# S4D layer and routed experts on one core: comparisons of places on 16-bit numbers, and another written order

## The chip, the cores and the metric

The kernel runs on one core of one Trainium2 chip. The metric is the time of one execution on the device in microseconds. The core has five engines that run beside each other, each with its own queue of instructions: TensorE (products; in the profile PE, its weight loads PEld), VectorE (DVE), ScalarE (ACT), GpSimd (POOL, here for gathers and scatters by index) and SyncE (SP, which issues the other transfers). Sixteen DMA engines move the data.

## The reference

Two layers with a residual each, on 2048 tokens of 512 channels. The first is a state-space convolution (S4D), computed in the reference with an FFT; the second sends each token to the best one of eight experts.

```python
def _A_ref(u, log_A_real, A_imag, C_real, C_imag, log_dt, D_skip):
    ...
    P = jnp.exp((A * dt[:, None])[:, :, None] * pos[None, None, :])
    K = 2.0 * jnp.einsum("dn,dnl->dl", C, P).real
    ...
    return y + u * D_skip[None, None, :]

def _B_ref(x, wg, w1, w2):
    gates = _softmax(xt @ wg, axis=-1)
    topk_idx = jnp.argsort(-gates, -1)[:, :K]      # K = 1
    ...
    h = _gelu(jnp.einsum("nd,edf->nef", xt, w1))
    y = jnp.einsum("nef,efd->ned", h, w2)
    out = jnp.einsum("ne,ned->nd", cw, y)

h = x + _A_ref(_layernorm(x), ...)
h2 = h + _B_ref(_layernorm(h), B_wg, B_w1, B_w2)
```

## The kernel before

**Stages.** The front (0 to about 125 us) loads the input in four pieces (l_x), takes the statistics of each token (u_stats, u_mean, u_dev, u_var, u_std, u_rstd), writes the normalised input (u_norm) and transforms it in two steps (u_s1, u_s2), while VectorE and ScalarE build the first tables of the convolution's kernel (t_e, t_f, t_vf, t_wi, t_wr and others). The main part goes over four blocks of 128 channels. For each block it finishes the tables, multiplies them out (t_kg, t_kt), transforms the result (c_s1, c_ev1, c_s2), multiplies with the transformed input that it loads from DRAM (c_load, c_z), transforms back (c_ia, c_ys), and sends the result through DRAM for a change of layout: c_yst writes it to yd_scratch, c_y1 loads it in four pieces, c_ib does the last small transform, c_add (L781) adds the residual. The finished block goes to DRAM (r_hd, into hd_scratch), and TensorE adds its share to the router's products (r_tr, r_ev, r_lg).

**The router.** When the last block is done, r_le and r_lt bring the products of tokens and experts into the right layout, and r_a finds each token's expert (oh). r_ag, r_sd and r_rs finish the mean and the reciprocal deviation of each token (the tile val), and r_vs (L1097) writes val into the last four columns of hd_scratch, four numbers in each of 2048 rows. r_p1, r_p1e and r_p2 count the tokens of each expert that stand ahead of each token. For the expert that runs first, r_c0, r_B0, r_t0 and r_i0 turn these counts into the list of its tokens: place p of the list is found by comparing the low part of each token's place (lo0) with 0 to 127 (is_lo, L1167), which gives a table B of zeros and ones for 16 tokens per partition, in two halves of 1024 comparisons, and by multiplying B with the tokens' numbers on TensorE (L1176). r_i0 (L1180) writes the index gi0. m_ga (L1285) gathers the token rows with it. Later r_c, r_M, r_B, r_tb and r_ix do the same for all experts; r_B uses the same is_lo, and o_b (L1258) a comparison of its own.

**The experts.** Each expert has up to 288 tokens in up to three chunks. m_ln (L1327) normalises the gathered rows (hn), m_tr (L1333) transposes them on TensorE, m_xh (L1340) and m_xl (L1345) split them into a high and a low part. Weights come in pieces of 512 KB (m_w1 L1365, m_w2 L1369), ScalarE takes their high part (m_h, L1373), VectorE the low part (m_l, L1377). m_g1 (L1386 to L1388) forms the first product from three products of the parts, m_ge, m_gh (L1394) and m_gl (L1398) apply gelu and split again, m_g2 forms the second product. The result is scattered to the output rows.

**What sets the order.** Each step is added as a task with an engine, an estimated cost, what it reads and what it writes (`plan.add`, called `at`). The table ORD gives every task's place, written out by hand as one list of 2045 places; ON says for some tasks whether VectorE (V) or ScalarE (A) does them; FILL puts idle products (L950) ahead of some tasks of TensorE. The program is issued in the order of ORD, so each engine's queue is in that order, and an instruction waits in its queue until what it reads is there and the buffer that it writes is free. The lists r= and w= in the calls decide only which buffer of a ring a task takes; the waits follow from the tiles themselves.

Buffers that matter here: c_y1's loads of blocks 0 to 2 share one buffer (y1), block 3's results three (ys3), the expert's r1 and r2 three each.

Of the kernel before, what the change touches and what calls it, by code (L numbers as in the profile page):

```python
# [22 lines left out]
KR = 3  # L23
# [62 lines left out]
def _dram(ap, dims, off=0):  # L86
# [40 lines left out]
    't_tb': [91, 115, 135, 169, 277, 310, 324, 350, 435, 466, 486, 510, 625, 659, 684, 720],
    't_trig': [96, 120, 138, 171, 288, 312, 328, 352, 443, 469, 491, 517, 635, 663, 689, 726],
    'r_sw': [98],
    't_wi': [103, 123, 149, 180, 295, 318, 339, 367, 453, 473, 498, 544, 642, 668, 700, 734],  # L130
    't_vb': [104, 105, 126, 153, 205, 294, 316, 340, 430, 452, 475, 497, 612, 622, 671, 694],
    't_vt': [107, 112, 131, 162, 212, 298, 320, 346, 454, 462, 477, 501, 631, 645, 675, 696],
    't_wr': [108, 128, 160, 203, 301, 322, 345, 373, 458, 481, 505, 553, 651, 678, 711, 741],
# [3 lines left out]
    't_vp': [113, 117, 145, 167, 239, 308, 354, 357, 464, 468, 531, 539, 637, 664, 717, 727],  # L137
    'r_swe': [116],
    't_kg': [119, 134, 165, 210, 311, 334, 361, 380, 470, 489, 538, 559, 660, 687, 728, 749],
    't_kt': [122, 142, 185, 272, 330, 342, 366, 388, 472, 496, 543, 583, 666, 693, 735, 758],  # L140
    't_d': [127, 144, 194, 278, 335, 344, 371, 419, 494, 504, 565, 589, 677, 730, 740, 761],
    'u_s2': [157, 146, 148, 154, 179, 172, 183, 163, 223, 197, 206, 204, 238, 231, 219, 192, 254, 241, 262, 250, 286, 283, 266, 274, 292,
        299, 309, 305, 315, 296, 302, 289],
    'u_ev2': [164, 151, 152, 158, 184, 178, 188, 173, 234, 200, 209, 213, 245, 236, 226, 198, 261, 247, 268, 255, 290, 287, 273, 280,
        297, 303, 314, 313, 319, 300, 306, 293],
    'u_st': [168, 161, 186, 191, 237, 215, 248, 229, 265, 271, 291, 282, 304, 317, 321, 307],
    'open_main': [323],
    'c_load': [369, 376, 325, 331, 329, 401, 416, 411, 456, 546, 524, 446, 485, 512, 503, 434, 585, 640, 638, 680, 670, 582, 652, 595,
        699, 719, 706, 748, 747, 752, 755, 762],
    'c_s1': [326, 338, 353, 347, 455, 437, 445, 463, 615, 597, 579, 607, 710, 733, 742, 763],  # L150
    'c_x': [327, 333, 534, 556, 713, 729, 765, 754],
    'c_ev1': [332, 337, 341, 343, 356, 355, 351, 349, 459, 461, 442, 441, 449, 450, 471, 467, 619, 618, 601, 602, 587, 591, 610, 611,
        715, 714, 739, 737, 743, 744, 767, 768],
    'm_load': [336],
    'c_s2': [386, 391, 360, 375, 358, 412, 433, 424, 478, 572, 555, 483, 502, 528, 525, 474, 621, 656, 650, 703, 681, 623, 673, 628, 775,
        791, 813, 782, 770, 796, 785, 800],
    'c_z': [398, 396, 362, 381, 363, 422, 444, 432, 487, 578, 562, 492, 509, 566, 529, 479, 624, 661, 658, 709, 690, 627, 686, 634, 781,
# [750 lines left out]
def moe(tc, plan, env, cst, wg, w1, w2, out):  # L908
# [143 lines left out]
    def r_cb(ev):  # L1052
        ev(cb[:, 0:264], t_["rt"][:, 0:264])
# [605 lines left out]
```

## Time and profile before

| what | us |
|---|---|
| median of 3 runs (736.88, 738.35, 738.35) | 738.35 |
| the profiled execution | 737.27 |
| its span, first to last instruction | 735.5 |
| TensorE busy | 662.1 |
| VectorE busy | 567.0 |
| ScalarE busy | 457.7 |
| GpSimd busy | 81.2 |

Durations and starts are those of the one profiled execution; its time is the span and what lies around it. A row of a timeline has the start and the length in us, the engine, the line, the operation, the tiles (out<-in), the shapes, the count, and in brackets how long the engine was idle ahead of it and what ended that. A row of a group has the count, then total busy time and mean ns of one, then the idle time. A row of the chain has start, length and what held the end at that time; an "SPq" in it is SyncE's issue of a transfer, "DMA" the transfer. TensorE's clock is a share of full speed.

### The profile page before, as it was taken

How to read it: one execution, taken by the hardware profiler on the slowest of the kernel's cores; microseconds unless marked ns; L12 is line 12 of the kernel's file. 1: busy time of each engine (PE TensorE's matmuls, PEld its weight loads, DVE VectorE, ACT ScalarE, POOL GpSimd, SP SyncE). 2: the span in 40 equal slices, each digit the busy share in tenths (PEclk: the TensorE clock that was granted, in tenths of full speed). 3: DMA queues.
4: the chain of work that ended last, by engine and by line, in shares of the span. 5: the costliest groups of instructions: out<-in, count | busy, mean ns of one | idle time of the engine just before them, and what ended most of it. 6: DMA issues, size and time to landing. Idle time of an engine off the chain costs nothing.

```text
span 735.5 us, 20126 instructions
## 1 busy us (share of the span) xinstructions
PE 662.1 (90%) x8280; PEld 583.3 (79%) x8280; DVE 567.0 (77%) x1065; ACT 457.7 (62%) x915; POOL 81.2 (11%) x68
## 2 busy tenths in 40 slices
PE   3788998998889997798679999999999999999995
PEld 1346887777778876594369999999999999998884
DVE  7999998889999999473689865766676767666752
ACT  7899999859975976211535545554555456566651
POOL 0000000000000000000106031050220403132201
PEclk9699999999999999999889999999999999999998
DMA  9993134665585687898747466466564656676620
GB/s 192 194 213 52 68 138 152 223 254 166 160 254 167 197 264 240 240 275 251 181 144 230 144 204 179 148 201 197 159 219 146 213 190 227 180 240 208 197 88 27
DMA packets 138344, 136.46 MB, mean 186 GB/s; under 512 B 42153, under 2 KB 108333, under 8 KB 137866
## 3 DMA queue, kind: packets, MB, share of 16 engines
q1 hardware_dynamic: 134666, 126.48, 59.3%
q0 software_dynamic: 3584, 8.67, 3.4%
q8 instruction: 66, 1.08, 0.6%
q14 instruction: 28, 0.23, 0.1%
HBM read 109.90 MB, written 29.59 MB: 190 GB/s over the span
## 4 chain that ended last, share of the span: by engine, by line
PE 45%; DVE 17%; issue 17%; DMA 12%; ACT 2%; SPq 2%; POOL 2%; POOLq 1%; DVEq 0%; ACTq 0%
DMA yd_scratch<-ys 5%; PE ps_s L1386 5%; PE ps_s L1387 5%; PE ps_s L1388 5%; DMA y<-yd_scratch 4%; PE ps_kk L1418 2%; PE ps_kk L543 2%; PE ps_ga L1418 2%; PE ps_kk L1420 2%; PE ps_ga L1420 2%; PE ps_kk L1419 2%; PE ps_ga L1419 2%; PE pk L674 2%; PE ps_s L524 2%; PE ps_pl L950 2%
## 5 line engine op out<-in xcount | busy, mean ns | idle before, releaser
L1377 DVE TENSOR_TENSOR l<-r,h 128x1024 fp32r<-128x1024 f32 x112 | 136.6, 1222 | 50.3 <-ACT h L1373 48.6
L1373 ACT CAST h<-r 128x1024 fp32r<-128x1024 f32 x112 | 117.5, 1049 | 82.6 <-PE ps_s L1388 39.2
L1386 PE MATMUL ps_s<-xh,h 128*128 128x288 f32 (+5 forms) x448 | 129.4, 289 | 0.0
L1388 PE MATMUL ps_s<-xl,h 128*128 128x288 f32 (+5 forms) x448 | 128.1, 286 | 0.0
L1387 PE MATMUL ps_s<-xh,l 128*128 128x288 f32 (+5 forms) x448 | 127.8, 285 | 0.2 <-DVE l L1377 0.2
L1391 ACT ACTIVATE g<-ps_s 128x288 f32<-128x288 f32 (+5 forms) x112 | 43.7, 390 | 68.9 <-PE ps_s L1388 49.2
L1387 PEld LDWEIGHTS ps_s<-xh,l 128*128 128x128 f32 x448 | 84.8, 189 | 1.9 <-DVE l L1377 0.4
L1386 PEld LDWEIGHTS ps_s<-xh,h 128*128 128x128 f32 x448 | 84.4, 188 | 2.1
L1388 PEld LDWEIGHTS ps_s<-xl,h 128*128 128x128 f32 x448 | 84.5, 189 | 0.0
L1398 DVE TENSOR_TENSOR gl<-g,gh 128x288 fp32r<-128x288 f32 (+5 forms) x112 | 46.9, 430 | 21.7 <-ACT gh L1394 20.1
L741 PE MATMUL ps_ga<-u,mi 128*128 128x128 f32 x256 | 51.0, 281 | 5.1 <-DVE u L734 2.7
L611 ACT ACTIVATE e<-alp 128x128 f32<-128x128 f32 x256 | 53.3, 310 | 3.1 <-PE pk L674 3.1
L950 PE MATMUL ps_pl<-ident 128*128 128x512 f32 (+1 forms) x152 | 52.8, 494 | 0.0
L1278 POOL DMA_INDIRECT out_dram<-ot,si x21 | 26.0, 1237 | 221.6 <-DVE ot L1435 217.5
L742 PE MATMUL ps_ga<-u,mi 128*128 128x128 f32 x256 | 49.5, 275 | 0.0
L741 PEld LDWEIGHTS ps_ga<-u,mi 128*128 128x128 f32 x256 | 38.8, 191 | 9.8 <-DVE u L734 2.4
L950 PEld LDWEIGHTS ps_pl<-ident 128*128 128x128 f32 x152 | 27.2, 212 | 24.1 <-issue 23.4
L734 DVE TENSOR_TENSOR u<-ps_kk,u 128x1024 f32<-128x1024 f32 x32 | 38.4, 1216 | 6.3 <-PE ps_kk L543 6.2
L1418 PE MATMUL ps_kk<-gh,h 128*128 128x288 f32 (+2 forms) x140 | 41.8, 299 | 0.0
L1418 PE MATMUL ps_ga<-gh,h 128*128 128x288 f32 (+2 forms) x140 | 40.9, 292 | 0.0
L1420 PE MATMUL ps_kk<-gl,h 128*128 128x288 f32 (+2 forms) x140 | 40.9, 292 | 0.0
L1420 PE MATMUL ps_ga<-gl,h 128*128 128x288 f32 (+2 forms) x140 | 40.8, 292 | 0.0
(286 smaller groups left out, 1608.4 us busy)
## 6 DMA issues: line engine op xcount, KB each, us to landing
r<-in_B_w_dram SPq DMA_DIRECT2D x112, 512.0 KB
u<-ud_scratch SPq DMA_DIRECT2D x32, 512.0 KB
ud_scratch<-xn SPq DMA_DIRECT2D x16, 512.0 KB
yd_scratch<-ys SPq DMA_DIRECT2D x32, 256.0 KB
y<-yd_scratch SPq DMA_DIRECT2D x16, 512.0 KB
xu<-in_A_u_dram SPq DMA_DIRECT2D x16, 256.0 KB
xd_scratch<-in_A_u_dram SPq DMA_DIRECT2D x8, 512.0 KB
xr<-xd_scratch SPq DMA_DIRECT2D x6, 512.0 KB
```

The source lines that it names most:

```text
L611: A.activation(tb[blk, "e"][:, l // 2, :, l % 2], par(alp, blk), AF.Exp, scale=float(l))
L741: T.matmul(pa[:, c], mi[:, 4 * rc + rr, 64:192], z[:, 0, c], start=True, stop=False)
L742: T.matmul(pa[:, c], mi[:, 4 * rc + rr, 0:128], z[:, 1, c], start=False, stop=True)
L950: T.matmul(p[:, 0:128 * k], w, _view(ident, [[0, k], [1, 128]]), start=first, stop=True, skip_group_check=True)
L1373: A.copy(tile_(("h" + n, e, f), list(r.shape), F32R, pool="wp", name="h" + n, bufs=2), r)
L1377: V.tensor_tensor(tile_(("l" + n, e, f), list(r.shape), F32R, pool="wp", name="l" + n, bufs=2), r, t_["h" + n, e, f].bitcast(F32), op=OP.s ...
L1386: T.matmul(o[:, 0:CAPS[e]], a, xh, start=c == 0, stop=False)
L1387: T.matmul(o[:, 0:CAPS[e]], b, xh, start=False, stop=False)
L1388: T.matmul(o[:, 0:CAPS[e]], a, xl, start=False, stop=c == 3)
L1398: V.tensor_tensor(tile_(("gl", e, f), [128, CAP], F32R, name="gl", bufs=3)[:, 0:n], t_["g", e, f][:, 0:n], t_["gh", e, f][:, 0:n].bitcast( ...
L1418: T.matmul(o, a, gh, start=f == 0, stop=False)
L1420: T.matmul(o, a, gl, start=False, stop=f == 13)
```

## The change

1. The comparisons of is_lo work on 16-bit numbers. lo and lo0 are stored as bf16; a new tile ir holds 0 to 127, each eight times, in bf16, made once by a new ScalarE step r_ir; and B has the tokens innermost instead of the places, so that the three operands are read and written in runs of eight neighbouring 16-bit numbers. TensorE then reads its weights from B with a step of 16 elements. o_b keeps its comparison.

2. Around the first gather VectorE's order is another one. m_l(0, 0, "1") moves from behind the first m_ln to a place ahead of the gather, behind r_a; r_p1e, r_k0, and only then r_rs follow it, and r_vs comes after close_main. Its weight load, m_w1(0, 0), moves ahead of three r_hd on SyncE. Behind the gather the order is m_ln 0, m_ln 1, m_xh 0, m_ln 2, m_xl 0, m_hold, m_xl 1, m_xl 2, r_c (before: m_ln 0, m_l, m_xh 0, m_ln 1, m_ln 2, m_xl 0, r_c, m_xl 1, m_xl 2). The idle products ahead of m_tr 1 go, those ahead of m_g1 0 are four in place of seven.

3. The order of the tasks ahead of that, in the front and in the main part, is written anew too, with ON and FILL. From place 1080 on it is the old one, shifted by the one new task. Of the parts that the prediction speaks of: the last u_norm of VectorE stands ahead of t_wi 0; t_kg 15 stands ahead of c_ib 8; on SyncE the end of the convolution reads

```
before: ... c_load31 r_hd8 c_x6 l_const c_y1 9 r_hd10 c_yst28 r_ld0 r_ld2 c_yst27 c_yst24 c_yst25 c_yst29
        c_yst30 c_yst31 c_yst26 c_y1 11 r_hd9 c_y1 12 13 14 15 r_hd11 m_w2 0 r_hd13 r_hd14 m_w1 0 r_hd12 r_hd15 r_vs
after:  ... c_load31 l_const r_ld2 c_yst29 c_y1 11 r_hd10 r_ld3 c_yst27 c_yst24 c_yst25 c_y1 9 r_hd11 c_yst28
        c_yst31 c_yst26 c_yst30 r_hd9 c_y1 12 13 14 15 m_w2 0 m_w1 0 r_hd14 r_hd12 r_hd13 r_hd15 r_vs
```

The diff, without most of ORD:

```diff
-    'm_l': [924, 943, 939, 954, 962, 990, 967, ...
+    'm_l': [898, 950, 941, 956, 965, 991, 969, ...
-    'r_rs': [896],
-    'r_k0': [897],
-    'r_vs': [899],
     'r_p1e': [900],
+    'r_k0': [901],
+    'r_rs': [902],
+    'r_vs': [905],
-    ... ('m_tr', 0): 11, ('m_tr', 1): 4, ('m_g1', 0): 7}
+    ... ('m_tr', 0): 11, ('m_g1', 0): 4}
...
+        sm("ir", [128, PR, 8], BF16)
...
+    def r_ir():
+        A.copy(t_["ir"], _view(rc["iota"], [[1, PR], [0, 8]]))
...
     def r_c():
-        pos, hi, lo, h2 = (sm(n, [128, 16]) for n in ("pos", "hi", "lo", "h2"))
+        pos, hi, h2 = (sm(n, [128, 16]) for n in ("pos", "hi", "h2"))
+        lo = sm("lo", [128, 16], BF16)
...
     def r_c0():
-        hi, lo, a3 = sm("hi0", [128, 16]), sm("lo0", [128, 16]), sm("a30", [128, 16, KR], BF16)
+        hi, lo, a3 = sm("hi0", [128, 16]), sm("lo0", [128, 16], BF16), sm("a30", [128, 16, KR], BF16)
...
     def is_lo(lo, h):
         if "B" not in t_:
-            sm("B", [128, 16, PR], BF16)
-        V.tensor_tensor(t_["B"][:, 8 * h:8 * h + 8], _view(t_[lo], [[1, 8], [0, PR]], 8 * h), _view(rc["iota"], [[0, 8], [1, PR]]), op=OP.is_equal)
+            sm("B", [128, PR, 16], BF16)
+        V.tensor_tensor(t_["B"][:, :, 8 * h:8 * h + 8], _view(t_[lo], [[0, PR], [1, 8]], 8 * h), t_["ir"], op=OP.is_equal)
...
-            T.matmul(t_["p0"][0:PR, 0:2 * KR], t_["B"][:, k], ...
+            T.matmul(t_["p0"][0:PR, 0:2 * KR], t_["B"][:, :, k], ...
...
-            T.matmul(t_["pt"][0:PR, 0:2 * NT], t_["B"][:, k], ...
+            T.matmul(t_["pt"][0:PR, 0:2 * NT], t_["B"][:, :, k], ...
...
+        at("A", 1.1, r_ir, r=["rc_/0"], w=["ir/0"])
...
+        at("S", 1.46, m_w1, 0, 0, r=["hw/0/o", "yl/0"], w=["r1/0"])
+        at("A", 0.98, m_h, 0, 0, "1", r=["r1/0"], w=["h1/0", "hc1/0"])
+        at("V", 1.18, m_l, 0, 0, "1", r=["r1/0", "h1/0"], w=["l1/0"])
         for e in range(E):
...
-                for n, fn in (("1", m_w1), ("2", m_w2)):
+                for n, fn in (("1", m_w1), ("2", m_w2))[(e, f) == (0, 0):]:
```

The other lines of the diff change estimated costs and the lists r= and w= of the same calls.

More of the change, by code (lines that the diff above doesn't have):

```diff
@@ L139 @@
[L139 to L145, printed above, removed]
@@ new lines @@
+    'l_m2': [42],
+    't_r6': [45, 126, 199, 431],
+    'l_wg': [46],
+    't_f6': [48, 137, 211, 437],
+    't_ep': [49, 153, 359, 529],
+    'u_mean': [50, 86],
+    't_r': [51, 192, 372, 549],
+    'u_dev': [54, 87],
+    't_f': [56, 62, 64, 68, 84, 89, 230, 234, 239, 246, 253, 259, 380, 403, 406, 416, 419, 426, 555, 561, 583, 592, 609, 619],
+    'u_var': [57, 90],
+    't_va': [58, 140, 213, 350, 409, 516, 567, 692],
+    'l_rest': [59],
+    'p_at': [60],
+    'u_std': [65, 91],
+    'u_rstd': [66, 93],
@@ L276 @@
-    'o_s': [1116],
-    'm_sc': [1117, 1125, 1129, 1263, 1268, 1272, 1410, 1414, 1416, 1558, 1562, 1567, 1695, 1699, 1704, 1818, 1821, 1948, 1951, 2042, 2043],
-    'm_dr': [1147, 1292, 1437, 1586, 1722, 1840, 1968, 2044],
+    'r_st': [789, 778, 807, 824],
+    'r_tk': [802],
+    'r_cb': [803],
+    'r_ir': [805],
+    'r_ag': [856, 863, 878, 888],
[3 rows of a table added]
+    'r_sd': [864, 871, 882, 895],
[3 rows of a table added]
+    'r_le': [869, 881, 887, 892],
+    'r_lt': [875, 886, 891, 894],
+    'm_h': [896, 890, 923, 925, 949, 982, 960, 1005, 986, 1031, 1010, 1048, 1035, 1062, 1052, 1082, 1086, 1099, 1105, 1136, 1128, 1157,
[5 rows of a table added]
@@ new lines @@
+    'r_a': [893, 897],
+    'm_l': [898, 950, 941, 956, 965, 991, 969, 1008, 997, 1033, 1019, 1053, 1039, 1069, 1077, 1083, 1091, 1103, 1109, 1141, 1132, 1164,
[8 rows of a table added]
+    'r_rs': [902],
+    'r_p2': [903],
+    'close_main': [904],
+    'r_vs': [905],
+    'r_c0': [906],
+    'r_c8': [907],
+    'r_B0': [908, 909],
+    'r_t0': [910, 914],
+    'r_ca': [911],
+    'r_s1': [912],
+    'r_i0': [918],
+    'r_ex': [919],
+    'm_ga': [920, 921, 922, 977, 983, 987, 1133, 1138, 1143, 1276, 1282, 1287, 1421, 1427, 1431, 1572, 1578, 1708, 1714, 1826, 1832],
@@ new lines @@
+    'm_hold': [934],
+    'r_c': [939],
[6 rows of a table added]
+    'r_B': [943, 951],
+    'm_ge': [945, 947, 964, 970, 979, 992, 1000, 1018, 1024, 1038, 1046, 1051, 1076, 1085, 1094, 1108, 1120, 1131, 1142, 1152, 1163,
[5 rows of a table added]
+    'r_M': [946],
+    'r_tb': [952, 958],
+    'm_gh': [954, 963, 971, 975, 984, 994, 1007, 1020, 1032, 1041, 1049, 1055, 1078, 1087, 1095, 1110, 1123, 1135, 1144, 1156, 1165,
[5 rows of a table added]
+    'm_gl': [957, 966, 976, 978, 988, 1012, 1016, 1023, 1036, 1042, 1056, 1067, 1079, 1089, 1096, 1111, 1129, 1137, 1145, 1158, 1167,
[5 rows of a table added]
@@ L295 @@
 }
[L296 to L300 removed]
+FILL = {('p_tr', 2): 19, ('u_mean', 0): 2, ('u_var', 0): 2, ('p_tr', 3): 2, ('u_mean', 1): 29, ('u_var', 1): 3, ('r_sw', 0): 9,
[3 rows of a table added]
+    ('r_lg', 7): 2, ('c_s1', 15): 1, ('r_tr', 9): 3, ('c_ib', 12): 6, ('m_tr', 0): 11, ('m_g1', 0): 4}
 EV = 0.49, 0.61
```

256 lines of the change are left out of this document (110 added, 146 removed), and 93 rows, old and new, of tables (FILL, ORD).

## The prediction

> **What bounds the kernel now.** I read the page's busy slices first, then busy time by stretch, the chain that ended last, VectorE and GpSimd in order of time around the first gather, and costs by group.
>
> ```profile
> span 735.5 us, 20126 instructions
> PE   3788998998889997798679999999999999999995
> DVE  7999998889999999473689865766676767666752
> ```
>
> The next view has, for each stretch of time, its length, the busy time of TensorE's products, its weight loads, VectorE, ScalarE and GpSimd, TensorE's clock, the DMA engines' busy share and GB/s.
>
> ```profile
> 326.00:330.00 4.00, 3.43 (x30) 3.24 (x29) 3.11 (x9) 0.96 (x3) 0.00 (x0) 1.00 0.78 238
> 330.00:334.00 4.00, 4.00 (x36) 3.56 (x35) 1.52 (x2) 0.72 (x2) 0.00 (x0) 1.00 0.60 168
> ...
> 338.00:342.00 4.00, 2.52 (x12) 0.94 (x11) 0.71 (x2) 0.00 (x0) 0.00 (x0) 1.00 0.96 264
> 342.00:346.00 4.00, 2.42 (x9) 0.66 (x8) 0.85 (x4) 0.59 (x1) 0.00 (x0) 0.79 0.98 322
> ```
>
> ```profile
> 371.00:377.00 6.00, 5.63 (x23) 3.62 (x24) 5.73 (x15) 1.93 (x3) 0.00 (x0) 0.66 0.00 0
> 377.00:393.00 16.00, 15.79 (x130) 15.25 (x129) 15.62 (x36) 7.45 (x14) 2.69 (x3) 1.00 0.70 215
> 393.00:500.00 107.00, 107.00 (x828) 106.40 (x827) 78.04 (x162) 57.38 (x97) 30.53 (x25) 1.00 0.59 182
> ```
>
> From 393 us on TensorE is busy 107.00 of 107, and the written order from there on is the old one. So whatever moves the start of the experts moves the end by as much. The hole in the busy digits lies ahead of it, in 333 to 377 us. The chain shows who holds that stretch (start, length, what):
>
> ```profile
> 334.24 2.56 DMA yd_scratch<-ys
> 336.88 7.32 DMA y<-yd_scratch
> 344.24 1.92 PE ps_s L778 x4
> ...
> 357.74 0.33 SPq L1097
> 358.12 5.97 DMA r<-in_B_w_dram
> ...
> 364.62 6.03 DMA rows<-hd_scratch,r_gi
> 370.68 0.56 DVE hn L1327
> ...
> 385.00 1.15 DVE l L1377
> 386.19 0.40 PE ps_s L1387
> ```
>
> Three parts: two transfers (334.24 to 344.24), the first gather with its wait (357.74 to 370.68), and VectorE from the first hn to the l that ends at 386.15, after which TensorE takes over.
>
> **What the gather waits for.** The chain names a weight load, but the gather reads no weights. It reads its index (r_gi, L1180) and the rows of hd_scratch, whose last four columns L1097 writes; and L1097's issue is the step ahead in the chain. VectorE's and GpSimd's rows, in order of time:
>
> ```profile
> 357.21 0.25 DVE L1044 RECIPROCAL r_val<-r_val 128x16 f32<-128x16 f32 x1
> 357.38 0.14 DVE L1152 TENSOR_TENSOR r_k<-r_rt,r_oh 128x32 f32<-128x32 f32 x1
> 357.57 0.16 DVE L1107 CAST r_cnt<-ps_kg 128x1 bf16<-128x1 f32 x1
> ...
> 361.97 0.16 DVE L1180 TENSOR_REDUCE r_gi<-ps_kg 128x3 int32<-128x6 f32 x1
> ...
> 372.49 0.69 DVE L1340 CAST xh<-ps_kg 128x512 fp32r<-128x512 f32 x1
> 373.10 0.98 DVE L1327 TENSOR_SCALAR hn<-rows 128x512 f32<-128x512 f32 x2
> ...
> 388.60 0.35 DVE L1203 TENSOR_REDUCE r_gi<-r_ge 128x24 int32<-128x192 f32 x1
> ```
>
> ```profile
> 389.70 0.96 POOL L1285 DMA_INDIRECT rows<-hd_scratch,r_gi  x1 [21.68 <-PE ps_ga L1420]
> ```
>
> The second expert's index is done at 388.95 and its gather begins 0.75 us later. The first index is done at 362.13, so by the index alone the first gather would begin at 362.9; it begins at 364.62. I conclude that the write of r_val decides, and that the index has 1.7 us of slack.
>
> **The change, part by part** (positive is slower).
>
> *r_rs behind the first m_l.* The reciprocal (L1044) that L1097 sends now has m_l(0, 0), r_p1e (L1107) and r_k0 (L1152) ahead of it. m_l takes 1.15 us by the row at 385.00; the small ones 0.19 and 0.17 from start to start. So L1097 is issued 1.5 us later, and with it the four weight loads queued behind it on SyncE; its landing, the gather and the rows follow: **+1.5**, with ends of 1.2 (if the small ones overlap) and 1.8 (if m_l waits for its h).
>
> [...]
>
> *The comparisons ahead of the gather (r_B0)* and the later start of r_c0 behind m_l both lie on the way to the index: the one saves, the other costs about a microsecond, and 1.7 us of slack cover either: **0**. Were that cover gone, they would count with their sum, about -0.2.
>
> *The comparisons behind it (r_B) and the order of m_ln.* The price, by groups of equal instructions (total, mean ns of one, idle before):
>
> ```profile
> L1167 DVE TENSOR_TENSOR r_B<-r_lo,r_rt 128x1024 bf16<-128x1024 f32 x4 | 4.8, 1215 | 0.0
> ...
> L1398 DVE TENSOR_TENSOR gl<-g,gh 128x288 fp32r<-128x288 f32 x5 | 2.2, 450 | 0.0
> ...
> L1188 DVE TENSOR_TENSOR r_M<-r_oh,r_ax 128x384 bf16<-128x384 bf16 x2 | 1.0, 550 | 0.0
> ...
> L1394 DVE CAST gh<-g 128x288 fp32r<-128x288 f32 x3 | 0.9, 303 | 0.0
> ```
>
> No row has 16-bit tiles read in runs of eight. Among the rows the same 288 elements cost 450 ns, or 303 where the instruction has one source; the 147 ns between them scale to 523 over 1024 elements, so 692 ns at best. Against it stands r_M, all in 16 bits and not fast: 384 elements in 550 ns. But r_M repeats an operand in its innermost step, as r_B does now and will not. So 692 to 1215 ns; I take 692, a saving of 0.52 each. I exclude a loss: the number of elements is the same.
>
> [...]
>
> Once the rows land, VectorE runs hn, then an l while TensorE transposes, then xh at 372.49, 1.81 us behind the first hn, and goes on without a gap to 386.15. The new order puts m_ln(1) where that l stood. Both are hidden by the transposes, so l's leaving wins nothing; what is won is that m_ln(1), half of 0.98 us, no longer stands behind xh. With two comparisons: -0.49 - 1.04 = **-1.53** (ends: -0.5 and -1.6). r_c's place behind the last xl lets TensorE start its first m_g1 some 1.6 us sooner but leaves VectorE's sum as it is; r_c and the comparisons are then covered by TensorE's first products only in part, and VectorE stays late.
>
> *TensorE.* In 371 to 377 its clock is 0.66 of full. With fewer transposes and fillers ahead, the first products may still find the low clock: 0 to 0.8 us for half an m_g1, largely hidden behind VectorE's pace: **+0.2**. The 32 products that use r_B as weights now read it with a step of 16 elements:
>
> ```profile
> L674 PEld LDWEIGHTS pk<-wi,vi 128*32 128x32 f32 x1024 | 32.0, 141 | 6.2 <-issue 3.4 <-DVE vi L650 1.5 <-DVE kt L678 0.2
> ...
> L1008 PEld LDWEIGHTS ps_pl<-ys,wgp 128*32 128x32 f32 x128 | 2.7, 110 | 4.2 <-issue 2.6 <-ACT ys L1000 0.8 <-ACT r_ls L1014 0.2
> ```
>
> The upper row reads with a wide step, the lower without: 31 ns each, 0.5 us for the sixteen behind the gather, hidden while VectorE is late: **0**. r_ir is one copy of 1024 elements on ScalarE, about a microsecond, right behind the first of these rows; it ends before the second, whose 2.70 us of idle time wait for a DMA: **0**.
>
> ```profile
> 322.44 0.41 ACT L1053 CAST r_cb<-r_rt 128x264 bf16<-128x264 f32 x1 [7.24 <-DMA r_rt<-const_rt_dram]
> 325.56 0.58 ACT L747 COPY ys<-ps_ga 128x512 f32<-128x512 f32 x1 [2.70 <-DMA yd_scratch<-ys]
> ```
>
> *The tail of the convolution.* The new order reaches further than its name: all queues differ up to the router. One move lies on the chain. Ahead of block 3's four y loads SyncE now issues block 2's last one (c_y1 11):
>
> ```profile
> 334.70 0.55 SPq L773 DMA_DIRECT2D y<-yd_scratch  x1
> 335.34 0.57 SPq L1022 DMA_DIRECT2D hd_scratch<-xr  x1
> 336.88 3.71 SPq L773 DMA_DIRECT2D y<-yd_scratch  x4
> ```
>
> The first row is that load, and the 7.32 us of the first of the four contain it: 0.52 MB at the 264 to 322 GB/s of 338 to 346 us are about 1.8 us. The new order issues it, and an hd write, before the last yd writes, at 326 to 334 us, where the DMA engines are idle for 0.22 and 0.40 of four microseconds each, 2.5 us in all. They fit: **-1.8**, with ends of 0 and -2.4 (the hd write too).
>
> *The front.* The last u_norm moves ahead of t_wi and its 2.3 us, so the first u_s1 may start up to 1.3 us earlier:
>
> ```profile
> 55.38 1.20 DVE L513 TENSOR_SCALAR xn<-xu,mr 128x128 f32<-128x128 f32 x4
> ```
>
> ```profile
> 56.72 1.28 PE L524 MATMUL ps_s<-s1u,xn 64*64 64x64 f32 x64 [2.88 <-DVE xn L513]
> ```
>
> But then t_wi, and what TensorE's t_kg waits for, come about as much later; VectorE's work is the same. I count **0**, within 1.3 either way.
>
> **Sum.** +1.5 - 1.53 + 0.2 - 1.8 = -1.6 us. The profiled execution took 737.27 us, 1.8 outside its span of 735.5; it would take 735.7. It lies within the runs (736.88 to 738.35), 1.1 below their median, so I forecast a median of 738.35 - 1.6 = 736.7 us, 0.22% faster. About 0.2%, 1.5 us, is what a measurement of this kernel can tell from no change.
>
> **Rivals.** *The gather follows its index.* [...] Against: the 1.7 us by which the gather missed its index. Then +1.5 becomes the -0.2 named above: -3.3, 735.1 us. Chance 0.17.
>
> *The tail stays where it is*, because the last yd write lands later by what the moved load took. For it: the DMA engines are at 0.78 and more just before. Then -1.6 becomes +0.2: 738.5 us. Chance 0.23.
>
> *Slower: a y load among the last yd writes.* In the new order c_y1 9 stands on SyncE between two groups of block 3's yd writes. With a single buffer for these loads it must wait until TensorE has finished c_ib 11, and the writes behind it wait as well; their three buffers then hold up c_ys, and c_ys TensorE. Price: the load's 1.8 us on the last write, with nothing saved: +0.2 + 1.8 = +2.0, 740.3 us. It decides from the point where that load still moves when the last two writes are issued. For it: the 2.56 us that the last write took are short, since nothing else moved. Against: the free 2.5 us. Chance 0.22.
>
> That the comparisons stay at 1215 ns belongs in each case: it adds 1.0.
>
> **How the numbers follow.** The forecast has 0.38, and the front's 1.3 us either way blurs all four. Of the forecast about 0.6 falls on faster and the rest mostly on same; the index rival is nearly all faster, the resting tail mostly same, the slower rival slower but for a fifth: 0.43, 0.31 and 0.26. The range goes from the index rival with the front's gain (735.1 - 1.1 = 734.0) to the slower rival (740.2), the forecast's own from 735.2 to 738.2.
>
> **What would show it.** L1097 issued some 1.5 us farther behind the last r_oh, and the gather no nearer to that r_oh although r_gi is ready sooner; r_B at about 690 ns; from the first hn to the l for the third m_g1 pair 13.9 us in place of 15.5; the first of the four y loads landing some 5.5 us after issue. The forecast is wrong if the gather follows r_gi within 0.8 us, if r_B stays near 1215 ns, or if the y loads keep their 7.3 us.

## The result, and the profile after

| | before | after |
|---|---|---|
| median, us | 737.68 (736.88 to 738.35, 4 runs) | 748.03 (747.49 to 749.72, 4 runs) |
| ratio, 95% interval | | 1.0146 (1.0116 to 1.0176) |
| profiled execution, us (span) | 737.27 (735.5) | 749.72 (747.9) |
| mean clock of TensorE in it | 0.971 | 0.950 |

The kernel became 1.5% slower, 10.35 us. The forecast of 736.7 was wrong, and so was the range up to 740.2. Every ratio here and below is to runs of the kernel before that were taken beside that run (so it is not the quotient of two medians of the table), and it leaves out runs more than 1.5% above the fastest of their kernel (two of e1 at 746.4, one of e14 at 752.5, one of e18 at 763.6 us), while the medians count them. The page after, busy tenths in 40 slices of 18.7 us, with the row of TensorE's granted clock:

```profile
span 747.9 us, 20106 instructions
PE   3569898898897988699669999999999999999995
DVE  7899998799898988575748975666776767776752
PEclk9579999999999999899869999999999999999998
```

The filled part from slice 23 on looks as before; it starts later. The chain of waits in the stretch that the prediction worked on (rows of "issue" below 0.1 us are left out):

```profile
350.04 6.81 DMA y<-yd_scratch
...
370.13 0.57 SPq L1102
370.75 5.36 DMA r<-in_B_w_dram
376.15 6.51 DMA rows<-hd_scratch,r_gi
382.68 0.56 DVE hn L1333
...
386.31 2.00 PE ps_kk L951 x2
388.31 0.24 PE ps_s L1392
...
390.70 0.13 PE ps_s L1393
```

And the comparisons:

```profile
L1173 DVE TENSOR_TENSOR r_B<-r_lo,r_ir 128x1024 bf16<-128x1024 bf16 x4 | 2.7, 686 | 0.0
```

All these steps are 11 to 13 us later than before, and they already start so. Laid along the milestones of both profiled executions (us): the last c_ia starts at 333.3 before and 346.2 after, **+12.9**; from there to the last c_ib 17.95 and 16.10 (-1.85); to the issue of the write of r_val 6.27 and 7.84 (+1.57); to the gather 7.13 and 6.02 (-1.11); to the first hn 6.06 and 6.53 (+0.47); to the first write of out 61.29 and 61.84 (+0.55); to the end 303.5 and 303.4. The sum is +12.4, the difference of the spans. The loss lies ahead of the last c_ia: 1.7 us of it are there when the first c_ia starts (158.7 and 160.4), and the rest is made in the convolution's main part, which the prediction had passed over with the words "all queues differ up to the router".

Where in it? Busy time by stretches of 20 us, before and then after (columns as in the prediction: PE, weight loads, DVE, ACT, POOL, TensorE's clock, DMA share, GB/s):

```profile
200.00:220.00 20.00, 18.47 (x252) 15.48 (x252) 19.70 (x25) 15.91 (x22) 0.00 (x0) 1.00 0.75 222
240.00:260.00 20.00, 18.32 (x306) 15.09 (x305) 18.99 (x21) 19.47 (x48) 0.00 (x0) 1.00 0.66 202
260.00:280.00 20.00, 19.46 (x377) 16.83 (x377) 18.95 (x24) 15.38 (x19) 0.00 (x0) 1.00 0.81 248
300.00:320.00 20.00, 15.82 (x294) 13.63 (x291) 10.75 (x25) 2.34 (x4) 1.15 (x1) 1.00 0.98 270
```

```profile
200.00:220.00 20.00, 18.04 (x247) 14.69 (x239) 16.70 (x22) 13.11 (x15) 0.00 (x0) 0.91 0.55 159
240.00:260.00 20.00, 18.39 (x352) 16.15 (x352) 16.80 (x20) 16.01 (x56) 0.00 (x0) 0.91 0.47 155
260.00:280.00 20.00, 17.89 (x244) 15.43 (x243) 17.22 (x19) 14.77 (x18) 0.00 (x0) 0.91 0.75 206
300.00:320.00 20.00, 13.33 (x438) 9.77 (x429) 9.88 (x19) 3.61 (x8) 0.00 (x0) 0.83 0.82 205
```

VectorE, busy 19 of 20 us before, loses 1.7 to 3 us in the first three of these stretches, and TensorE's clock falls in four. 0.91 over 20 us is one window of 3.41 us at half speed (the first has 0.50 from 202.82 to 206.24 us), 0.83 is two: five windows, up to 1.7 us each of TensorE's time. (Before has none between its first and its last c_ia.) What TensorE waited for between 140 and 350 us without a releaser in the profile ("issue"; total, times, longest), before and after:

```profile
PE pk L674 <- issue: 4.1, 2, 2.6
PE ps_s L524 <- issue: 2.1, 1, 2.1
PE ps_ga L741 <- issue: 1.7, 1, 1.7
```

```profile
PE pk L675 <- issue: 4.5, 1, 4.5
PE ps_ga L742 <- issue: 3.8, 2, 2.2
PE ps_pl L951 <- issue: 3.6, 1, 3.6
PE ps_s L779 <- issue: 2.0, 1, 2.0
PE ps_ga L998 <- issue: 1.9, 1, 1.9
PE ps_kk L544 <- issue: 0.5, 1, 0.5
```

7.9 us before, 16.3 after. An engine that waits for nothing visible, in the middle of the products of one t_kg (pk), may wait for its own instructions. The trace has a DMA queue of the kind "instruction" with 66 packets of 16 KB, one for every 252 recorded instructions of TensorE; e6 below, with 18,683 records in place of 16,651, has 74. After, TensorE has eleven gaps of over 1 us between 100 us and the last c_ia, 23.4 us in all; five of them, 13.8 us, are "issue" and end 1.2 to 1.6 us behind the end of one of these packets. Before it is four, 7.9 us. Their places settle what they are: counted in TensorE's records from the start, they lie whole multiples of 256 apart (within one). In all 20 profiles, whatever the order, 64 of the 67 "issue" gaps of over 1 us in that part end so behind a packet and stand at such a place; of the 116 gaps with a releaser one does. These 64 are late code. The largest, 4.51 us from 309.99 in t_kg 15, ends 1.48 us behind the packet that landed at 313.02. What SyncE had issued just ahead, before (t_kg 15 from 300.5 us) and after (from 308.0):

```profile
294.99 0.55 SPq L773 DMA_DIRECT2D y<-yd_scratch  x1
295.60 1.94 SPq L727 DMA_DIRECT2D u<-ud_scratch  x2
300.53 0.54 SPq L773 DMA_DIRECT2D y<-yd_scratch  x1
```

```profile
303.60 0.55 SPq L774 DMA_DIRECT2D y<-yd_scratch  x1
305.69 0.33 SPq L761 DMA_DIRECT2D xr<-xd_scratch  x1
306.11 1.17 SPq L728 DMA_DIRECT2D u<-ud_scratch  x2
307.33 0.66 SPq L761 DMA_DIRECT2D h<-xd_scratch  x1
308.04 0.94 SPq L985 DMA_DIRECT2D hr<-hd_scratch  x1
309.03 1.30 SPq L761 DMA_DIRECT2D h<-xd_scratch  x1
```

So the **theory of the code**: the new order puts loads of 0.5 MB close ahead of TensorE's densest products; its code comes late behind them, TensorE stands for 2 to 5 us, and then works at the low clock. Rivals: the loss is made around the gather after all; the clock fell by chance in that one execution; VectorE's order, not the code, holds TensorE up.

### The profile page after: what moved, and what is told of

Read it like the earlier page. It is cut to its first block, busy times and chain, and to the rows that moved or that the text cites. A ratio compares the mean times of both kernels' runs of the same rounds, so it can differ in the third digit from the quotient of the medians.

```text
span 747.9 us, 20106 instructions
## 1 busy us (share of the span) xinstructions
PE 665.4 (89%) x8274; PEld 591.0 (79%) x8274; DVE 569.7 (76%) x1071; ACT 458.0 (61%) x910; POOL 79.1 (11%) x68
## 4 chain that ended last, share of the span: by engine, by line
PE 53%; issue 17%; DVE 12%; DMA 9%; ACT 3%; SPq 2%; POOL 2%; POOLq 1%; DVEq 0%; ACTq 0%
PE ps_s L1392 5%; PE ps_s L1393 5%; PE ps_s L1394 5%; PE ps_kk L544 5%; PE pk L675 4%; DMA y<-yd_scratch 3%; PE ps_ga L742 3%; PE ps_ga L743 3%; PE ps_kk L1424 2%; PE ps_kk L1426 2%; PE ps_ga L1426 2%; PE ps_kk L1425 2%; PE ps_ga L1424 2%; PE ps_ga L1425 2%; PE ps_s L779 2%
## 5 line engine op out<-in xcount | busy, mean ns | idle before, releaser
L742 PE MATMUL ps_ga<-u,mi 128*128 128x128 f32 x256 | 52.5, 287 | 4.8 <-issue 3.8
L951 PE MATMUL ps_pl<-ident 128*128 128x128 f32 (+1 forms) x156 | 50.1, 463 | 3.6 <-issue 3.6
L743 PE MATMUL ps_ga<-u,mi 128*128 128x128 f32 x256 | 50.7, 281 | 0.0
L742 PEld LDWEIGHTS ps_ga<-u,mi 128*128 128x128 f32 x256 | 40.2, 198 | 6.0 <-issue 4.4
L743 PEld LDWEIGHTS ps_ga<-u,mi 128*128 128x128 f32 x256 | 40.2, 198 | 1.7 <-issue 1.7
L544 PEld LDWEIGHTS ps_kk<-ks,m 128*128 128x128 f32 x256 | 33.0, 203 | 10.1 <-issue 7.0
```

The costliest lines, as they stand in the source:

```text
L544: T.matmul(ps[:, 128 * rr:128 * rr + 128], m2[:, 4 * rc + rr, :], src[:, 4 * rc + rr, :], start=True, stop=True)
L742: T.matmul(pa[:, c], mi[:, 4 * rc + rr, 64:192], z[:, 0, c], start=True, stop=False)
L743: T.matmul(pa[:, c], mi[:, 4 * rc + rr, 0:128], z[:, 1, c], start=False, stop=True)
L951: T.matmul(p[:, 0:128 * k], w, _view(ident, [[0, k], [1, 128]]), start=first, stop=True, skip_group_check=True)
```

## The experiments

Orders are put together from the two kernels: the first tasks in the order of one, all others in the order of the other, each with its kernel's engines and fillers. The table has every run but e6 and e7. "Stretch" is from block 2's first c_ia to block 3's, "gap" the longest wait of TensorE in t_kg 15, "rest" from the last c_ia to the end; these and the first c_ia are of the profiled execution, in us.

| run | median, us | ratio to before (95%) | first c_ia | stretch | gap | rest |
|---|---|---|---|---|---|---|
| before | 737.68 | | 158.7 | 58.8 | 1.55 | 402.2 |
| after | 748.03 | 1.0146 (1.0116, 1.0176) | 160.4 | 63.9 | 4.51 | 401.8 |
| e1 old to task 740 | 740.09 | 1.0038 (1.0001, 1.0076) | 158.0 | 62.2 | 4.84 | 401.0 |
| e2 new to task 740 | 747.68 | 1.0143 (1.0090, 1.0196) | 163.6 | 63.6 | 1.50 | 400.5 |
| e3 comparisons alone | 737.88 | 1.0033 (1.0002, 1.0064) | 161.5 | 57.5 | 1.27 | 400.2 |
| e4 after, again | 746.67 | one run | 162.3 | 61.5 | 5.35 | 403.1 |
| e5 front alone | 741.29 | 1.0051 (1.0007, 1.0095) | 162.0 | 58.3 | under 1 | 401.0 |
| e8 old from 560 to 740 | 744.28 | 1.0111 (1.0048, 1.0174) | 164.0 | 59.7 | 2.59 | 401.4 |
| e9 traffic, 2 KB | 737.43 | 1.0025 (0.9996, 1.0053) | 159.6 | 56.9 | 1.01 | 399.2 |
| e10 e1 and fillers | 741.59 | 1.0087 (1.0058, 1.0117) | 157.2 | 61.1 | 5.10 | 401.6 |
| e11 e10 and write first | 738.87 | 1.0011 (0.9984, 1.0038) | 162.6 | 61.0 | 4.85 | 396.9 |
| e12 before and fillers | 736.71 | 0.9995 (0.9964, 1.0025) | 162.0 | 56.2 | 1.01 | 399.8 |
| e13 old to the router | 737.16 | 0.9997 (0.9968, 1.0026) | 156.9 | 55.5 | 1.26 | 398.3 |
| e14 loads together | 744.34 | 1.0081 (1.0041, 1.0122) | 158.9 | 66.1 | 6.22 | 400.2 |
| e15 loads apart | 760.27 | 1.0314 (1.0271, 1.0358) | 164.3 | 59.2 | 4.26 | 403.7 |
| e16 traffic, 8 KB | 742.52 | one run | 164.5 | 55.3 | under 1 | 401.3 |
| e17 after, 2 KB pieces | 745.46 | 1.0117 (1.0069, 1.0164) | 161.8 | 54.9 | 1.50 | 403.4 |
| e18 e13, 2 KB pieces | 738.24 | 1.0004 (0.9976, 1.0033) | 158.9 | 55.5 | 1.09 | 397.6 |

One execution says little to a microsecond or two: the 102 runs of the kernel before that were taken beside these runs lie between 731.9 and 743.6 us. The quarter with the lowest mean clock (0.966) averages 739.1 us, the one with the highest (0.975) 735.5.

**e1 and e2: which half of the change costs.**

```diff
 after.py, order of tasks
-new[0:740] + new[740:]
+old[0:740] + new[740:]
```

> The kernel after, with the old order (and the old engines and fillers) of the front and of the convolution for the first 740 tasks of the order; the tail of the convolution, the router and the experts stay new, with the 16-bit comparisons. Theory one (the loss lies in the new order of the convolution's main part): the last c_ia, 12.9 us later in the profile after, comes back to within 1.5 us of before, and the whole runs at 737.7 - 1.8 (tail) + 1.5 (write of r_val) - 0.5 = about 737, 735 to 739. Theory two (the loss is made around the first gather: the write of r_val, the comparisons, VectorE's order there): 745 to 748 us, as after.

```diff
 before.py, order of tasks
-old[0:740] + old[740:]
+new[0:740] + old[740:]
```

> The kernel before, with only the new order (and the new engines and fillers) of the front and of the convolution for the first 740 tasks of the order; the tail, the router, the experts and the comparisons stay old. Theory one (the main part's order costs): 737.7 + 12.9 = about 750, 748 to 752. Theory two (the loss is made around the first gather): 737 to 739, as before.

e2 carries the whole loss without any change behind task 740; e1, with everything new behind it, loses 0.4%. Theory two is out. But e1 did not come to before: its last c_ia starts 2.7 us later (expected: within 1.5), its time lies above the 735 to 739 expected, and its gap in t_kg 15 is 4.84 us. The moves of the loads around t_kg 15 stand just behind task 740, so e1 still has them. And e2, with the old order there, has a gap of only 1.50 in t_kg 15: the whole loss comes without the largest gap. What e2 has is more of the others (TensorE's longest waits for "issue", 140 to 350 us, 15.2 us in all):

```profile
PE ps_pl L960 <- issue: 6.6, 2, 4.9
PE ps_ga L751 <- issue: 2.9, 2, 2.1
PE ps_s L788 <- issue: 2.4, 1, 2.4
```

One thing that e2 carries was not taken apart: with the order go its engines and its idle products, and from the first c_ia to the last the idle products are busy for 15.4 us in e2 and 14.6 in after, where before has 12.2.

**e3: the comparisons alone.**

```diff
-V.tensor_tensor(t_["B"][:, 8 * h:8 * h + 8], _view(t_[lo], [[1, 8], [0, PR]], 8 * h), _view(rc["iota"], [[0, 8], [1, PR]]), op=OP.is_equal)
+V.tensor_tensor(t_["B"][:, :, 8 * h:8 * h + 8], _view(t_[lo], [[0, PR], [1, 8]], 8 * h), t_["ir"], op=OP.is_equal)
```

> The old order everywhere with the 16-bit comparisons and the one copy they need (r_ir, put behind r_cb). The prediction's own step: r_B falls from 1215 to about 690 ns, the two behind the gather save 0.5 us each on VectorE's way to the experts: 736.7. The rival (the comparisons are covered, or TensorE is what is late behind the gather): 737.7, no change; r_B at 1215 ns: no change either.

r_B takes 683 to 686 ns, and the kernel is not faster: 0.0 to 0.6% slower. From the first hn to the first write of out it took 62.7 us against 61.3, with the low clock until 6.8 us behind the hn against 4.4. In this run the time saved on VectorE does not reach the end.

**e4: after, unchanged, once more.**

> The kernel after, unchanged, for a second profiled execution. If the low-clock windows of TensorE between 160 and 345 us (five of 3.41 us in the first profile) come from the order of the work, they stand at the same places again, within a few us, and the last c_ia starts near 346 us; if they are a chance of one execution, others or none are there and the time differs by several us.

Half and half. Of the low windows only the two that begin near the end of the gap in t_kg 15 are there again (308 to 315 us; 312 to 319 in the first profile); the three at 203, 240 and 268 are not, and two stand at 147 to 154. So most of their places are chance, but the last pair goes with the gap, as it does in e1, e10, e11 and e14. But the time is 746.67, and the waits for "issue" from 140 to 350 us are there again, 15.1 us in all:

```profile
PE ps_pl L951 <- issue: 6.1, 2, 4.6
PE pk L675 <- issue: 5.4, 1, 5.4
```

**e5 and e8: front, first half, second half.**

```diff
 before.py, order of tasks
+new[0:322] + old[322:]
```

> The kernel before with only the new order of the front (the first 322 tasks, up to the opening of the main part). If the front is the cause of the loss: about +10 us, 746 to 748. If it shifts the start alone (the first c_ia was 1.7 us later in the profile after): +1 to +3. As the prediction had it: 0, within 1.3.

```diff
 after.py, order of tasks
+new[0:560] + old[560:740] + new[740:]
```

> The kernel after with the old order from task 560 to task 740 (the second half of the main part: blocks 2 and 3 and the tables of block 3); front, blocks 0 and 1, tail, router and experts stay new. If the stretch from block 2's first c_ia to block 3's (63.9 us after against 58.8 before) is where the order costs most, this one comes to 742 to 744; if the loss has come in by then (front and blocks 0 and 1, +7.1 us in the first profiles), 745 to 748.

The front alone costs 0.5% (0.1 to 1.0): 3.8 us, where the prediction had 0 within 1.3; the lower end, 0.5 us, does not exclude that. Its profile has no more late code than before (gaps of over 1 us: 4.4 us). Taking the second half back wins 2.5 us in the mean, which the intervals do not separate from nothing. The loss has no single place.

**e6 and e7: code or time.** Fillers ahead of eight tasks of block 2, once as many small products, once as few wide ones.

```diff
+FILL[("c_s2", 16..23)]: 64 products of 32 weight columns by 64   (e6)
+FILL[("c_s2", 16..23)]: 13 units of 128 columns                  (e7)
```

> The kernel before with 64 small extra products (32 columns of weights, 64 moved columns) ahead of each of the c_s2 tasks 16 to 23: 8 x 128 more instructions of TensorE in block 2, about four more fetches of code of 256 instructions, and 8 x 64 x 22 ns = 11 us of TensorE's time. The next run has the same time of TensorE with 8 x 4 wide products in their place. Theory of the code (TensorE stands where its code comes late behind other transfers, in 255 to 330 us): this one is 3 us or more slower than the wide one, and has more gaps of 1 to 4 us that end 1.1 to 1.6 us behind the end of a 16 KB code packet. Rival (code is not what TensorE waits for): the two are the same within 1.5 us.

> The kernel before with 13 filler units (three products of 512 columns and one of 128, 1.4 us) ahead of each of the c_s2 tasks 16 to 23: the same TensorE time as the run before, in 8 instructions a place and not 128. Theory of the code: 3 us or more faster than the run with the small products, since the fillers give each fetch of code more time; at most 11 us slower than before, and less where they fill gaps. Rival: as the small ones, within 1.5 us.

787.84 and 759.78 us (ratios 1.0716 and 1.0319). As a comparison of times the pair tells nothing: the 512 products are 1024 records, and one takes 57 ns, not the 22 ns expected (pk's 2048 records in before took 39.2 us, 19 ns each). The 1024 took 58.6 us of TensorE, more than the whole loss; the pair differs by its own time. At that pace the code even keeps up: the gaps of over 1 us behind late code fall from 5.8 to 1.2 us in the stretch. In e7, whose fillers ran as 13 products of 128 columns a place and not as the four wide ones expected, they rise to 8.8. Both go against the theory as it was put there, which had more gaps in e6 and fewer in e7.

**e9 and e16: transfers that nobody waits for**, put where the DMA engines are idle, from 67 us on.

```diff
+for k in range(12): dma_start(junk[k], kt)         # 256 KB, pieces of 2 KB  (e9)
+dma_start(junk, kt); for k in range(6): dma_start(junk2[k], x[k])   # 512 KB, pieces of 8 KB  (e16)
```

> The kernel before with 12 writes of 256 KB (the first table's kt, to a DRAM tensor that nobody reads) issued by SyncE once that table is done, at about 66 us, where the DMA engines are busy for a sixth of the time and no gap of TensorE between 60 and 100 us is longer than 0.9 us. No engine waits for these writes. Theory of the code: TensorE's 16 KB code packets, now 1 to 2 us behind the instruction that asks for them, come up to 10 us late behind the 3 MB; TensorE shows gaps of 2 us or more between 66 and 80 us that end 1.1 to 1.6 us behind a code packet, and the first c_ia starts 1.5 us or more later. Rival: no such gaps, the first c_ia within 1.5 us of the old order's other runs (158.0 to 161.5).

> As e9_more_traffic, with one write of kt and then six copies of 0.5 MB from one DRAM tensor to another in pieces of 8 KB, the size of the pieces of h, in place of the 2 KB pieces of e9. If pieces of this size are what holds a code packet back: TensorE has a gap of 2 us or more between 66 and 85 us, ending 1.1 to 1.6 us behind a code packet. If it is not the size of the pieces: gaps of at most 1.3 us, as in e9.

TensorE's waits from 66 to 82 us in before, e9 and e16:

```profile
PE pk L674 <- issue: 0.6, 1, 0.6
```

```profile
PE pk L684 <- issue: 1.2, 1, 1.2
```

```profile
PE pk L684 <- issue: 2.8, 1, 2.8
```

All three lie at the same place of the same t_kg. e9 was to show 2 us or more and did not, with DMA engines busy for 0.93 to 0.99 of 68 to 76 us; its traffic hardly delayed the code (1.2 us, and e13, without any extra traffic, has 1.15 us at this place). As many bytes in pieces of 8 KB did: the gap is 2.84 us and ends 1.4 us behind its code packet. (e16 copies from DRAM and e9 from SBUF, so the size of the pieces is not the only difference.) For the "1 to 2 us behind the instruction that asks" of e9's expectation, before has this: its packets 1 to 11, from 62 to 107 us, end 1.6 to 3.2 us behind TensorE's record 256n + 152 (n the packet's number from 0, records from 1), and none of packets 1 to 64 begins ahead of that record. Which instruction asks was not shown.

**e14 and e15: the loads together, the loads apart.**

```diff
 before.py, order of tasks
 c_load 28, c_load 27,
+c_x 7, r_ld 3, r_ld 1, c_x 6,
 t_kg 15, c_y1 10, c_add 8, c_load 29, r_s4 0,
-c_x 7, r_ld 3, r_ld 1, c_x 6    (each from its place among the next 16 tasks)
```

> The kernel before with four of SyncE's loads of 0.5 MB (the h of c_x 7 and 6, the hr of r_ld 3 and 1) moved ahead of t_kg 15, so that they stand together ahead of c_y1 10, as the new order has them. Theory (big loads issued together make TensorE's code late, and the load of y that stands behind them): the stretch from block 2's first c_ia to block 3's grows from 56 to 59 us to 61 or more, with a gap of 3 us or more in TensorE's products of t_kg 15, and the time by 2 to 4 us. Rival: the places of these loads do not matter, 737.

TensorE's waits in e14, 295 to 320 us:

```profile
PE pk L683 <- issue: 9.1, 2, 6.2
```

Four loads moved by a few places in the old order make the longest gap of all, 6.22 us, lengthen the stretch to 66.1 us and cost 0.8% (0.4 to 1.2). What the time comes from is less clear than the gap: the chain of e14 runs through the load of y that stands behind the four, issued at 303.49 us, which took 15.14 us and ended only at 318.63, when the gap in t_kg 15 was 7 us past. Late y alone may be what costs here.

```diff
 after.py, order of tasks
-c_x 7, c_ib 8, t_kt 15, r_ld 1, c_x 6, t_d 15, r_lg 6, c_add 8, c_y1 10, r_ld 0, r_s4 0, c_s1 15, c_load 28
+c_ib 8, c_y1 10, t_kt 15, c_load 28, t_d 15, c_x 7, r_lg 6, c_add 8, c_load 30, r_s4 0, c_s1 15, r_ld 1
...
```

> The kernel after with the same loads (c_x 7 and 6, r_ld 1 and 0, c_load 28, 30, 31) moved behind c_y1 10 and spread as in the old order; nothing else of the order is changed. Theory: the gap of 4 to 5 us in t_kg 15 goes or falls below 2.5 us, the stretch from block 2 to block 3 falls by 2 to 4 us from 61.5 to 64, and the time to 744 to 746. Rival: 747 to 749 as after.

Mostly a miss. The stretch fell as expected, to 59.2, but the gap stayed at 4.26: y, xr and two u stood ahead of t_kg 15 just the same, so h and hr alone are not its cause. And SyncE, now waiting for c_ib 8 at c_y1 10, issued the other loads so late that TensorE stood 10.1 us in block 3.

**e17 and e18: the same loads in smaller pieces.** u and xr come in pieces of 4 KB, h in pieces of 8 KB.

```diff
-nc.sync.dma_start(u, _dram(ud, [[1024, 64], [0, 2], [1, 1024]], ...))
+for k in range(2):
+    nc.sync.dma_start(u[:, k], _dram(ud, [[1024, 64], [0, 2], [1, 512]], ... + 512 * k))
```

(and so for c_x, in two or four loads of 512 columns)

> The kernel after with the loads of u (pieces of 4 KB), xr (4 KB) and h (8 KB) each issued as two to four loads in pieces of 2 KB; the order, the bytes and the work are the same. Theory (a code packet waits behind the large pieces of the loads issued just ahead of it): the gap of 4 to 5 us in t_kg 15 and the one of 4 to 5 us ahead of block 0 (near 146 us) fall below 2.5 us, and the time falls by 3 us or more, to 745 or less. Rival (the bytes count, not their pieces): the gaps stay and the time is 747 to 750, as SyncE has more to issue.

TensorE's waits in e17, 140 to 350 us:

```profile
PE ps_s L781 <- DMA y<-yd_scratch: 10.4, 8, 4.5
PE ps_pl L953 <- issue: 2.8, 1, 2.8
PE ps_ga L743 <- issue: 1.8, 2, 1.5
PE pk L675 <- issue: 1.5, 1, 1.5
PE ps_ga L744 <- issue: 1.0, 1, 1.0
PE ps_kk L544 <- issue: 0.9, 1, 0.9
```

With the new order untouched, "issue" falls from 16.3 to 8.0 us, the gap in t_kg 15 from 4.5 to 1.5, the one near 146 us to 2.8 (expected: below 2.5), and the stretch from 63.9 to 54.9. The last c_ia starts at 338.7, against 346.2 and 341.7. Part of it comes back as waits for y, one of 4.49 us in block 3. The time is 745.46 (expected: 745 or less); its interval overlaps that of after, so a gain of 2 us is likely, not shown. The other side counts more: TensorE's waits for "issue" are back at the 7.9 us of before, and the kernel is still 1.2% slower. Part of that lies behind the first hn, where this profile has the clock low until 6.6 us behind it and takes 64.2 us to the first write of out, against 61.8 in after.

**e10 to e13: behind the convolution.**

```diff
-('m_tr', 0): 11
+('m_tr', 0): 28                        # e10 (on e1), e11, e13; e12 (on before)
-r_a 1, m_l 0, r_p1, r_p1e, r_k0, r_rs, r_p2, close_main, r_vs
+r_a 1, r_rs, r_vs, m_l 0, r_p1, r_p1e, r_k0, r_p2, close_main     # e11, e13
```

> As e1_main_old (old front and main part, new tail, router order and experts, 16-bit comparisons), with 28 filler units in place of 11 ahead of m_tr 0, while TensorE waits for the first rows. Theory (what the comparisons and the order of m_ln save is lost to TensorE's low clock, which in the new order lasts until 8 us behind the first hn): the clock is full from the first hn on, from the first hn to the first write of out takes 59 us in place of 61.9, and the time is 2 to 3 us below e1_main_old. Rival (VectorE is what sets the pace there, whatever the clock): 61.9 us from hn to the first write of out, no change.

> As e10_fill_new, with the reciprocal of r_val and the write of r_val ahead of the first m_l. By the prediction's term A (the gather follows the landing of that write, and m_l stands ahead of it): the write is issued 6.3 us behind the last c_ib and not 7.8, the gather begins 1.5 us sooner, and the time is 1.5 us below e10. If the gather follows the index: no change. With both, 400.5 - 3 = 397.5 us from the last c_ia to the end, about 3 us (0.4%) faster than before.

> The kernel before with 28 filler units in place of 11 ahead of m_tr 0 and nothing else. Theory of the clock: full clock from the first hn on (the old order has it 4.4 to 6.8 us behind), hn to the first write of out 61.3 us falls by 1 to 2. Rival (VectorE sets the pace): 61.3, no change.

> The whole old order up to the last r_a (front, convolution and tail), then the new order with the write of r_val ahead of the first m_l, the 16-bit comparisons, and 28 fillers ahead of m_tr 0. If what costs is the order before the router, and what gains is behind it: from the last c_ia to the end 397 us as in e11 (400.5 in the old order's runs), block 2 at the old order's 56 to 59 us, so about 3 us (0.4%) below before. If e11's gain was chance: no change.

e10 missed its condition: its fillers ended at 367.3 us, ahead of the first hn (368.8), and the clock was low until 8.2 us behind it. In e11 (first hn at 375.4) it was full. The two, around their first hn:

```profile
368.00:372.00 4.00, 2.29 (x13) 1.69 (x13) 2.93 (x7) 0.58 (x1) 0.00 (x0) 0.77 0.19 75
372.00:376.00 4.00, 4.00 (x12) 2.97 (x13) 3.86 (x11) 1.55 (x2) 0.00 (x0) 0.50 0.45 133
```

```profile
372.00:376.00 4.00, 3.73 (x9) 1.33 (x7) 0.55 (x1) 1.56 (x2) 0.68 (x1) 1.00 0.96 378
376.00:380.00 4.00, 3.16 (x19) 2.20 (x20) 3.45 (x10) 1.98 (x3) 0.00 (x0) 1.00 0.07 15
```

From the first hn to the first write of out: 62.5 us in e10, 59.7 in e11, 59.5 in e13, where the clock was full too. In the old order the full clock changes nothing (e12: 61.1 against 61.3); that VectorE, busy for 15.62 of the 16 us from 377 us on in before, sets the pace there is my reading. With the write ahead of m_l (e11), the reciprocal starts 6.22 us behind the last c_ib and not 7.53, and the gather follows the write as before, 6.1 us behind. From the last c_ia to the end e11 and e13 take 396.9 and 398.3 us, 1 to 4 us below the old order's other runs (399.2 to 401.3 without the first profile's 402.2). Whole runs do not show it: e13 lies within 0.3% of before either way, not the 0.4% below that were expected. e18 (e13 with the small pieces) was to be 2 us below e13; its waits for "issue" fell from 3.6 to 2.6 us, and its time is no better. e13 beats the kernel after by some 1.5%; a version that beats the kernel before was not found.

## Why the prediction was wrong, point by point

- **The gather follows the write of r_val** held. After, the index is done at 373.26 us and the gather begins 2.9 us later; in every run it begins 6.0 to 7.1 us behind that write's issue, and in e11 it came with the write. In the five profiles that have the landing of that write (e6, e7, e13, e14, e16) the gather begins 1.0 to 1.1 us behind it. **+1.5** for the place of m_l was right: 5.99 to 7.53 us, +1.54.
- **r_B at 692 ns** held (686), partly by luck: the 692 was worked out from rows on 32-bit numbers with one source and with two, in which nothing is read in 16 bits. Its place ahead of the gather costs and wins nothing, as said.
- **-1.53 behind the gather, +0.2 for TensorE's clock.** The first term exists, but only at full clock: 61.3 to 59.7 us in e11, and 61.1 (e12) to 59.5 (e13) with the same 28 idle products on both sides. The second was mis-sized. After, the low clock lasts until 7.9 us behind the first hn (4.4 before): two fillers on the chain take 2.00 us, and the products 0.24 us each until 390.7, then 0.13. Measured: 61.84 - (61.29 - 1.53), **+2.1** in place of +0.2. The prediction had seen the fillers ahead of the transposes fall away and taken VectorE's pace for a cover, and it was gone with the very term that it counted.
- **-1.8 in the tail** was a wrong reading that looks right. The tail did become 1.85 us shorter against the profile of before, but the y load still took 6.81 us; eight other runs with the old tail (e2, e3, e5, e9, e12, e13, e14, e16) have 15.4 to 16.7 us from the last c_ia to the last c_ib, where that one profile had 17.95, and after and e4 have 16.1 and 15.9. Behind the new order the term is worth nothing. Behind the old order it is worth about 1 us: e1, e10 and e11, with the new tail, have 14.8 to 14.9. I had built it on one execution.
- **"The front. ... I count 0, within 1.3 either way", and with it the whole order up to the router: this step failed.** The prediction put the whole new order ahead of the router, but for one load, at nothing. It cost 12.9 us in the first pair of profiles; in e4 and e2 the last c_ia starts 8 and 11 us behind the 333.8 that five runs of the old order (before, e3, e9, e12, e13) have in the mean, and e2 alone is 1.4% slower. Behind the last c_ia the two profiles differ by -0.4 us (402.2 and 401.8), where the prediction's terms sum to -1.6. I priced the moved instructions by who waits for their data; none of those prices is large. What I left out is that the order also sets which loads are under way when TensorE's next packet of code (252 recorded instructions) has to come in. I had written down the rows of "issue" ahead of pk (in the row of L674, 3.4 us) and used them for a weight load.
- The slower rival (a y load among the last yd writes) did not happen: it is another place and mechanism than the one that cost.

What is shown: the loss is made ahead of task 740 (e2); nearly all "issue" gaps of over 1 us ahead of the last c_ia (64 of 67) are late code, by their places in TensorE's instructions; the one in t_kg 15 follows the loads ahead of it (e14 makes it, e17 takes it away; in the table it is above 4 us with the new order of these loads and at most 1.55 with the old one, e8 at 2.59 in between). That large pieces hold the code back more than small ones rests on e17 and, with another source of the data, on e9 and e16.

What is not shown: that these gaps are the loss. The one in t_kg 15 is not: e2 has the whole loss with 1.50 us there, e11 almost none with 4.85. The sum of all such gaps goes with the loss better: 13.8, 14.0 and 14.4 us in after, e4 and e2, and 3.6 to 7.9 in the five runs of the old order. But e17 has 5.8 and is 1.2% slower, e11 has 9.3 and is not. The account of one pair of profiles, from the first c_ia to the last (before, then after):

```profile
158.68:333.28 174.60, 155.03 (x2887) 135.17 (x2884) 153.16 (x210) 111.53 (x250) 1.15 (x1) 1.00 0.72 214
160.40:346.18 185.78, 162.99 (x2894) 139.87 (x2892) 157.70 (x219) 111.36 (x247) 1.15 (x1) 0.95 0.71 206
```

The 11.2 us more are 8.0 of TensorE being busy, 6.8 of waits for "issue" (5.8 and 12.7), and 3.1 less of its other waits. The 8.0 fit five windows at half speed, up to 8.5 us, with the 2.4 us more of idle products among them; but no run set the clock, the idle products or VectorE's order alone, so how the loss divides stays open, and so do the 0.5% of the front and the loss between the first c_ia of block 0 and that of block 1 (3.3 us in this pair).

## What to carry to other kernels

A new order of the work is an edit of the kernel even where no instruction changes: compare the queues' order of loads against the dense stretches of TensorE. Test whether an "issue" gap in the middle of one task is late code by counting TensorE's instructions: here 64 of 67 such gaps stood at the same steps of 256 recorded instructions, in every order. A gap that is explained is not yet a loss that is explained: taking half of these waits away (e17) won about 2 us of 10, if anything. With loads in pieces of 2 KB (e17) TensorE waited 8.0 us for "issue" where it had waited 16.3 with pieces of 4 and 8 KB, at two to four issues for one. The gain on VectorE showed where TensorE had the full clock behind it (59.7 us from the first hn to the first write of out in e11) and not where the clock was low until 6.8 us behind the hn (62.7 in e3); and a term taken from one execution has to be looked up in a second one.

## What the hardware showed that I had not expected

- TensorE's instructions come by DMA while the kernel runs, in packets of 16 KB (66 packets for 16,632 records after), and TensorE resumes 1.2 to 1.6 us behind the end of a packet that was late (64 gaps in 20 profiles), always at a step of 256 records. Between 393 us and the end, with wide products, TensorE has no gap of over 1 us before and after; in the other runs the few that there are have a visible releaser.
- In both profiles, before and after, the clock changes on a grid of 3.41 us: every stretch at full or half speed, but the last, is a whole number of such windows long (1 to 104), and the grids of the two lie 0.46 of a window apart. After, the windows ahead of a low one between 160 and 345 us had TensorE busy for 0.28 to 0.43 of them; windows with 0.45 (before) and 0.51 kept the full clock, though others of before with 0.45 (ahead of 150 us) and 0.54 (ahead of 344 us) did not. Two of the low ones, from 202.82 and 240.37 us, followed a window with a single long gap, of 1.96 and 2.21 us.
- Two orders of one program, alike but for engines and idle products (e2 and before), differ by 1.4%, and one order by up to 1.6% from run to run (731.9 to 743.6 us).
